# One PSUM sum for a weight gradient of two layers, more tiles turned in the forward, and turned tiles stored from SyncE, in a fused forward and backward kernel

## The chip, the cores and the metric

The kernel runs on one core of a Trainium2 chip. The metric is the device time of one execution in microseconds (us). The core has five engines that run in parallel, each with its own static stream of instructions: TensorE (PE; its weight loads are counted as PEld), VectorE (DVE), ScalarE (ACT), GpSimd (POOL) and SyncE (SP). An engine takes its instructions in order, so one that waits holds all that are behind it. A DMA is issued by an engine: SyncE and ScalarE feed a hardware queue each (q1 and q10), GpSimd the software queue q0; all use the same 16 DMA engines.

## The reference

Two kinds of layers alternate, A, B, A, B, on a sequence of S = 2048 rows and D = 448 columns; the kernel returns the output and the gradients of all inputs.

```python
kv = shift_conv(k, shift_k) * v                     # layer A, kv is the same in both A layers
y  = irfft(rfft(kv) * rfft(ssm_k)) + kv * ssm_D     # causal convolution over the sequence
A(q) = q * y
B(x) = silu(x @ w1) @ w2                            # layer B, w1 448 x 1792, w2 1792 x 448
x = A_q
x = x + A(layernorm(x));  x = x + B(layernorm(x))   # B here: "layer 1", L == 0 in the code
x = x + A(layernorm(x));  x = x + B(layernorm(x))   # B here: "layer 2", L == 1 in the code
out = x;  grads = vjp(grad_out)                     # of A_q, A_k, A_v, A_shift_k, A_ssm_k, A_ssm_D, w1, w2
```

The gradient of w2 (gw2, output 8) is silu(h)^T times the gradient that arrives at the layer, summed over layers 1 and 2; gw1 (output 7) is the gradient of h, transposed, times the normalised input, summed over both layers as well.

## The kernel before, in words

The width F = 1792 is cut into 14 blocks of 128 (`NF`), the sequence into 16 blocks of 128 (`NT`) and, in the layers, into four chunks of 512 rows.

1. `_ssm_prefix` (to about 103 us) makes the convolution by Fourier transforms written as matmuls and stores the spectra in DRAM.
2. `Main.run` does the layers. For each chunk `h` makes h in two halves of seven blocks (L556), ScalarE makes tanh and silu from it (L560, L561), and VectorE and ScalarE make the slope dT (L566 to L570; for layer 2 the complement of the tanh term is made by the activation at L566, for layer 1 by VectorE). `out` multiplies by w2 (ps_o, L588). Layer 2 goes straight on to its backward: `g_pre` turns grad_out (gb loaded by SyncE), `ga` multiplies by w2 transposed (ps_g, L618) and makes ghT on ScalarE and VectorE (L624, L625), and `gn` multiplies by w1 transposed (ps_n, L659) and makes the layernorm's backward. When all four chunks of layer 2 are through, layer 1's backward follows chunk by chunk, with dTl, nb_l and na_l loaded by SyncE (`load_l0`).
3. `_ln` makes the layernorms: VectorE takes the statistics (L257 to L262, ln_ve last), GpSimd takes rstd from it (L264), VectorE makes ln_nmr (L266) and ScalarE the normalised rows (na, nb, L271). TensorE turns them (ps_t, L503).
4. silu(h), aT in the code, and ghT are kept for the weight gradients. They lie with the width on the partitions, but are wanted there with the sequence on the partitions. There are two ways. `store_plain` (L484) stores the tile as it is, from GpSimd, and the transpose is made when it is loaded again (`dma_start_transpose` in `_load_stat`). `store_turned` (L476 to L481) turns the tile in the forward with two DMA transposes from SyncE (of four and three blocks, L480) into `turned` (two buffers), and GpSimd stores that (L481). Half 0 of layer 1 is stored plain, half 1 and both halves of layer 2 turned; of ghT layer 1 plain, layer 2 turned.
5. `_wgrad_w2_first` makes layer 1's part of gw2: per block 16 matmuls (ps_d, L795) of a loaded stat tile (dstat) and mov2, the layer's gradient. ScalarE copies the sum (dpo, L804) and GpSimd stores it in fp32 in W2P_d (L805). Ten blocks are placed at the end of `Main`, four in the next stage.
6. `_ssm_suffix` makes the convolution's backward: stage 1 of the transform (ps_s, L209, with the constants M1s, loaded at L852 by GpSimd), transposes (ps_tr, L873), the product with the spectra per part cp = 0 to 6 (`spectrum`, `kernel_part`, `inverse`; kk_c holds the loaded spectra, L229 and L230 are the inverse transform), and the gradients gK, gkv, and gk. It ends at about 731 us. `kernel_part` also loads ksf (1.8 MB, at cp 2) and mov3 (1.8 MB, at cp 4).
7. `_wgrad_rest` makes layer 2's part of gw2 (its moving operand grad_out, dmov, loaded by SyncE) and adds the part in W2P_d to it (dpart, L816; DVE, L821), and then gw1: per block 32 matmuls, a copy (dout, L826), transposes (ps_dt) and a scaled copy (do7, L831).

A tile scheduler decides the static order of every engine when the kernel is built, from priorities and a cost model. Work of `_wgrad_w2_first` and `_wgrad_rest` has a low priority and so fills TensorE's gaps in the convolution's backward; `issue_after` sets only the earliest place. A tile with a `tag` and `bufs=n` takes one of n places in turn, and so waits for the last reader of what was there before. The PSUM banks are "mm" (two of two banks), "tr" (two) and "po" (two).

## Time and profile before

| what | value |
|---|---|
| median of 8 executions | 829.93 us (828.0 to 841.82) |
| the profiled execution | 836.9 us, span 835.1 us, mean granted TensorE clock 0.97 |
| software queue q0 (GpSimd) | 92.99 MB, 34.0% of 16 engines' span |
| stores of A_d and GH_d from turned (GpSimd) | 12 and 8, of 896 KB |
| loads of dstat from A_d (SyncE) | 21, of 512 KB, median 8.2 us to landing |
| ps_d, second products (L795, with dmov) | 448 matmuls, 99.0 us, mean 356 ns |
| last ps_n matmul, VectorE's end of the layers | 547.1 us, about 563.6 us |
| convolution's backward ends, gw1 | about 731 us, 736.9 to 830 us |

The page gives the busy time of each engine, the span in 40 slices, the DMA queues, a chain of work that ended last, and groups of instructions by line. A line of the timeline reads: start, length, engine, source line, operation, result<-operands, shape, count, and in brackets the idle time before and what ended it. The waits view gives for each engine and line what it waited for: us in total, times, longest. Times come from one execution.

### The profile page before, as it was taken

How to read it: one execution, taken by the hardware profiler on the slowest of the kernel's cores; microseconds unless marked ns; L12 is line 12 of the kernel's file. 1: busy time of each engine (PE TensorE's matmuls, PEld its weight loads, DVE VectorE, ACT ScalarE, POOL GpSimd, SP SyncE). 2: the span in 40 equal slices, each digit the busy share in tenths (PEclk: the TensorE clock that was granted, in tenths of full speed). 3: DMA queues.
4: the chain of work that ended last, by engine and by line, in shares of the span. 5: the costliest groups of instructions: out<-in, count | busy, mean ns of one | idle time of the engine just before them, and what ended most of it. 6: DMA issues, size and time to landing. Idle time of an engine off the chain costs nothing.

```text
span 835.1 us, 12887 instructions
## 1 busy us (share of the span) xinstructions
PE 759.1 (91%) x4921; PEld 414.3 (50%) x4950; DVE 570.1 (68%) x1252; ACT 455.5 (55%) x577; POOL 152.6 (18%) x225
## 2 busy tenths in 40 slices
PE   6998788999997989969999999998879899989997
PEld 4966443444443444424444444454546585445553
DVE  4789677999863896986968999992465467701000
ACT  4789776787956858568855533323435563200100
POOL 1143222232111012011101001112111142311111
PEclk9999898999998999989999999999998999999999
DMA  9269898776787759958799556499888969797771
GB/s 320 110 207 274 326 231 210 231 240 202 194 159 178 176 154 201 153 176 220 221 269 272 205 171 199 118 260 302 296 260 291 348 252 193 207 273 180 188 177 42
DMA packets 168875, 181.36 MB, mean 217 GB/s; under 512 B 135456, under 2 KB 139168, under 8 KB 167662
## 3 DMA queue, kind: packets, MB, share of 16 engines
q1 hardware_dynamic: 144768, 83.54, 41.2%
q0 software_dynamic: 22304, 92.99, 34.0%
q10 hardware_dynamic: 1742, 4.02, 2.1%
q8 instruction: 38, 0.62, 0.3%
q14 instruction: 23, 0.19, 0.1%
HBM read 69.85 MB, written 70.19 MB: 168 GB/s over the span
## 4 chain that ended last, share of the span: by engine, by line
issue 26%; DVE 23%; PE 19%; ACT 13%; DMA 12%; POOL 6%; SPq 0%; POOLq 0%; ACTq 0%; DVEq 0%
PE ps_d L795 4%; DMA out_dram<-gKD 3%; DVE lb_u L642 3%; DVE X L643 3%; DMA turned<-aT 2%; DVE lb_junk L639 2%; ACT aT L561 2%; PE ps_g L618 2%; DMA KB<-Z 2%; ACT dT L560 2%; ACT dT L566 2%; POOL rstd L264 2%; DMA dstat<-A_d 2%; ACT nb L271 2%; DVE dT L570 2%
## 5 line engine op out<-in xcount | busy, mean ns | idle before, releaser
L795 PEld LDWEIGHTS <-dstat 128*128 128x128 bf16 x896 | 87.1, 98 | 88.7 <-issue 7.5
L618 PE MATMUL ps_g<-gT,w2T 128*128 128x512 bf16 x432 | 103.3, 389 | 14.1 <-ACT ghT L624 13.0
L556 PE MATMUL ps_h<-nT,w1sb 112*128 112x512 bf16 x448 | 107.0, 385 | 4.1 <-ACT aT L561 2.5
L795 PE MATMUL ps_d<-dmov,dstat 128*128 128x448 bf16 x448 | 99.0, 356 | 7.3 <-DMA dstat<-A_d 4.7
L659 PE MATMUL ps_n<-w1T,ghT 128*128 128x448 bf16 x448 | 91.3, 352 | 5.7 <-ACT lb_u L661 3.7
L588 PE MATMUL ps_o<-w2sb,aT 128*128 128x448 bf16 x448 | 93.7, 355 | 1.5 <-DVE X L589 1.0
L795 PE MATMUL ps_d<-mov,dstat 128*128 128x448 bf16 x448 | 92.6, 355 | 0.2 <-DMA dstat<-A_d 0.2
L618 PEld LDWEIGHTS <-w2T 128*128 128x128 bf16 x448 | 44.6, 100 | 69.4 <-issue 21.2
L556 PEld LDWEIGHTS <-w1sb 112*128 112x128 bf16 x448 | 44.1, 99 | 58.7 <-issue 13.9
L624 ACT CAST ghT<-ps_g 128x1024 bf16<-128x1024 f32 (+1 forms) x64 | 55.9, 904 | 30.2 <-PE ps_g L618 25.5
L560 ACT ACTIVATE dT<-ps_h 128x1024 bf16<-128x1024 f32 (+1 forms) x64 | 59.1, 923 | 22.4 <-PE ps_h L556 21.5
L659 PEld LDWEIGHTS <-ghT 128*128 128x128 bf16 x448 | 42.7, 98 | 49.3 <-issue 6.1
L826 DVE CAST dout<-ps_d 128x448 bf16<-128x448 f32 x14 | 8.7, 625 | 83.4 <-PE ps_d L795 83.4
L588 PEld LDWEIGHTS <-aT 128*128 128x128 bf16 x448 | 42.9, 98 | 43.8 <-ACT aT L561 4.2
L561 ACT ACTIVATE aT<-ps_h 128x1024 bf16<-128x1024 f32 (+1 forms) x64 | 59.3, 926 | 0.0
L831 ACT ACTIVATE do<-ps_dt 112x512 bf16<-112x512 bf16 x14 | 8.4, 597 | 90.2 <-PE ps_dt L829 90.2
L229 PE MATMUL ps_v<-Gsb,pa 128*128 128x128 bf16 x336 | 45.5, 229 | 7.9 <-DVE pa L439 4.0
L661 ACT ACTIVATE lb_u<-ps_n,rhalf 128x448 f32<-128x448 f32 x32 | 20.5, 640 | 51.9 <-DVE gYb L669 22.0
L230 PE MATMUL ps_v<-Gsb,pb 128*128 128x128 bf16 x336 | 44.3, 229 | 2.2 <-DVE pb L440 1.6
L569 DVE TENSOR_TENSOR w1p<-w1p,aT 128x1024 bf16<-128x1024 bf16 (+1 forms) x64 | 39.6, 618 | 6.9 <-ACT aT L561 6.0
L570 DVE TENSOR_TENSOR dT<-w1p,dT 128x1024 bf16<-128x1024 bf16 (+1 forms) x64 | 39.5, 617 | 3.5 <-ACT dT L566 3.3
L566 ACT ACTIVATE dT<-dT 128x1024 bf16<-128x1024 bf16 (+1 forms) x32 | 30.6, 964 | 18.1 <-DVE lb_cc L641 17.8
(193 smaller groups left out, 1324.5 us busy)
## 6 DMA issues: line engine op xcount, KB each, us to landing
A_d<-turned POOLq DMA_DIRECT2D x12, 896.0 KB, 5.4
dstat<-A_d SPq DMA_DIRECT2D x21, 512.0 KB, 8.2
DT_d<-dT POOLq DMA_DIRECT2D x8, 896.0 KB, 5.2
GH_d<-turned POOLq DMA_DIRECT2D x8, 896.0 KB, 6.6
dTl<-DT_d SPq DMA_DIRECT2D x8, 896.0 KB, 6.4
GH_d<-ghT POOLq DMA_DIRECT2D x8, 896.0 KB, 7.1
dstat<-GH_d SPq DMA_DIRECT2D x14, 512.0 KB, 3.6
spec_K<-Z POOLq DMA_DIRECT2D x7, 512.0 KB, 7.8
```

What stands on the lines that cost most here:

```text
L229: nc.tensor.matmul(pv[:, i, :], lhsT=pa[:, i * P:(i + 1) * P], rhs=k.Gsb[:, ga, :], start=True, stop=False)
L230: nc.tensor.matmul(pv[:, i, :], lhsT=pb[:, i * P:(i + 1) * P], rhs=k.Gsb[:, gb, :], start=False, stop=True)
L556: nc.tensor.matmul(ps[:, u, :], lhsT=self.w1sb[:, dc, ft * P:(ft + 1) * P], rhs=nT[:DC, dc, :], start=(dc == 0), stop=(dc == ND - 1))
L560: nc.scalar.activation(tm, ps[:, 0:n, :], ACT.Tanh, scale=-0.5)
L561: nc.scalar.activation(a, ps[:, 0:n, :], ACT.Silu)
L566: nc.scalar.activation(tm, tm, ACT.Copy, scale=-1.0, bias=1.0)
L570: nc.vector.tensor_tensor(out=tm, in0=wv, in1=tm, op=ALU.add)
L588: i = nc.tensor.matmul(po[:, :D], lhsT=aT[ft // 7][0][:, ft % 7, tl * P:(tl + 1) * P], rhs=self.w2sb[:, ft, :], start=(ft == 0), stop=(ft ...
L618: nc.tensor.matmul(ps[:, u, :], lhsT=self.w2T[:, b, ft * P:(ft + 1) * P], rhs=gT[:, b, :], start=(b == 0), stop=(b == ND - 1))
L624: nc.scalar.copy(v, ps[:, u[0]:u[0] + len(u), :])
L659: nc.tensor.matmul(pn[:, :D], lhsT=ghT[ft // 7][:, ft % 7, tl * P:(tl + 1) * P], rhs=self.w1T[:, ft, :], start=(ft == 0), stop=(ft == NF - 1))
L795: nc.tensor.matmul(ps[:, :D], lhsT=st[:, t, :], rhs=movs[gi][:, t, :], start=(gi == 0 and t == 0), stop=(gi == len(groups) - 1 and t == NT ...
```

## The change: what it does

- The first store of layer 1's silu(h) keeps only four blocks plain; the other ten of the fourteen are turned in the forward (seven before). Half 0 of layer 1 is now stored as four plain blocks and one turned piece of three.
- `store_turned` issues its store from SyncE, right behind its transposes, and no longer from GpSimd.
- gw2 of both layers is one PSUM sum. The DRAM tile W2P_d, the copies, stores, loads and the addition are gone. A class `Wgrad` loads the stats of the four plain blocks while the layers still run (`open`, called twice in layer 1's backward), makes their layer 1 part at the end of `Main` (`hold`) and keeps the four sums in the banks "tr" and "po" until `w2` goes on with layer 2's part. The other ten blocks make both parts one after the other.
- grad_out for gw2 (mov1) is loaded on ScalarE's queue into the place of w2T; M1s and the odd kk_c and gK2 go into the place of w1T.
- ksf is loaded at cp 6 instead of cp 2, into the place "WB" instead of one of its own; mov3 and dmov give way to two movn tiles, loaded by GpSimd just ahead of gw1. gk has two buffers instead of three, dout three instead of four, do7 one instead of two, dstat (dp) three instead of two.
- The fourth thing that the change is said to do, layer 2's slope complement on ScalarE, has no line in the diff: L566 stands in both kernels.

The diff, cut to its core:

```diff
-    k.A0_d = (dram.tile([NF // 2, P, S], ...), dram.tile([P, NF // 2, NT, P], ...))
+    k.A0_d = (dram.tile([4, P, S], ...), dram.tile([P, NF - 4, NT, P], ...))
-    k.W2P_d = dram.tile([F, D], FP32, name="W2P_d")
...
+            k.mov1 = k.wt.tile([P, NT, D], BF16, name="mov1", tag="w2T")
+            nc.scalar.dma_start(out=k.mov1[:], in_=_pm(k.grad_out[0]))
+            k.M1sb = k.wt.tile([P, 16, 2, P], BF16, name="M1s", tag="w1T")
+            nc.gpsimd.dma_start(out=k.M1sb[:].rearrange("p a c k -> p (a c k)"), in_=k.m1_h.ap())
             with tc.issue_after(k.d0_load.ins):
-                _wgrad_w2_first(k, m.td, range(10))
+                k.wg.hold()
...
-        nc.gpsimd.dma_start(out=dst[:, 7 * hh:7 * hh + 7, 4 * c:4 * c + 4, :], in_=an[:])
+        nc.sync.dma_start(out=dst[:, f0 + lo:f0 + hi, 4 * c:4 * c + 4, :], in_=an[:, lo:hi])
...
-            self.store_plain(k.A0_d[0], aT, c, 0)
+            self.store_plain(k.A0_d[0], aT, c, 0, 4)
+            self.store_turned(k.A0_d[1], aT, c, 4, 7, -4)
...
+            if c < 2:
+                k.wg.open(self.td)
...
+    def stat(self, pool, tag, bufs, src, ft):
+        if pool is None or self.job % (bufs + 3) < 3:
+            st = k.dp.tile([P, NT, P], BF16, name="dstat", tag="dstat", bufs=3)
+        else:
+            st = pool.tile([P, NT, P], BF16, name="dstat", tag=tag, bufs=bufs)
+        self.job += 1
+        _load_stat(k, st, src, ft)
...
+    def open(self, pool):
+        for _ in range(2):
+            self.stats.append(self.stat(pool, "S", 2, self.k.A0_d, len(self.stats)))
+    def hold(self):
+        for ft, st in enumerate(self.stats):
+            ps = self.k.psum.tile([P, 512], FP32, name="ps_d", tag=("tr", "po")[ft // 2], bufs=2)
+            self.last = _wmm(self.k, ps, st, self.k.mov2, True, False)
+            self.held.append(ps)
+    def w2(self, pool, mov):
+        for ft in range(NF):
+            if ft < 4:
+                ps = self.held[ft]
+            else:
+                ps = self.k.psum.tile([P, 512], FP32, name="ps_d", tag="tr", bufs=2)
+                _wmm(k, ps, self.stat(pool, "dstat", 3, k.A0_d, ft), k.mov2, True, False)
+            _wmm(k, ps, self.stat(pool, "dstat", 3, k.A_d1, ft), mov, False, True)
+            o = pool.tile([P, D], BF16, name="dout", tag="dout", bufs=3)
+            nc.vector.tensor_copy(o[:], ps[:, :D])
...
-                if cp == 2:
+                if cp == 6:
                     tc.keep_in_program_order(nc.gpsimd.dma_start(out=ksf[:], in_=_pm(k.KS_d[:])))
-                if cp == 4:
-                    tc.keep_in_program_order(nc.gpsimd.dma_start(out=mov3[:], in_=_pm(k.N_d[3][:])))
...
-            gk = p2.tile([P, 2, D], BF16, name="gk", tag="gk", bufs=3)
+            gk = p2.tile([P, 2, D], BF16, name="gk", tag="gk", bufs=2)
...
-        _wgrad_rest(k, dp2, after, mov3)
+        es2.close()
+        with tc.issue_after(k.wg.last):
+            k.wg.w2(dp2, k.mov1)
+        p3 = pool("sp3")
+        mov = [p3.tile([P, NT, D], BF16, name=f"movn{i}") for i in range(2)]
+        for L in (1, 0):
+            nc.gpsimd.dma_start(out=mov[L][:], in_=_pm(k.N_d[2 * L + 1][:]))
+        k.wg.w1(dp2, mov)
```

## The prediction

> **What bounds the kernel now.** I read the busy totals first, then the 40 slices, the waits, and the timeline at the few places where TensorE stands still.

> ```profile
> PE 759.1 (91%) x4921; PEld 414.3 (50%) x4950; DVE 570.1 (68%) x1252; ACT 455.5 (55%) x577; POOL 152.6 (18%) x225
> ...
> PE   6998788999997989969999999998879899989997
> ...
> PEclk9999898999998999989999999999998999999999
> ```

> TensorE is busy 759.1 of 835.1 us; no other engine passes 68%. The change issues the same matmuls (896 of ps_d in both, and as many in all), so it pays only through idle time of TensorE or through its granted clock. Three stretches matter: the layers (to 547 us, the last ps_n matmul), the backward convolution (to 731) and the closing products (to 835). Summing TensorE's gaps over short windows from 547 to 830 gives 19.96 us, the large ones below.

> ```profile
> 576.01 0.54 PE L209 MATMUL ps_s<-gYb,M1s 128*128 128x448 bf16 x2 [2.83 <-ACT A1g L111]
> 625.69 0.55 PE L795 MATMUL ps_d<-dmov,dstat 128*128 128x448 bf16 x1 [3.86 <-DMA dstat<-A_d]
> 667.15 0.29 PE L229 MATMUL ps_v<-Gsb,pa 128*128 128x128 bf16 x1 [3.74 <-DVE pa L908]
> ```

> The bracket is the idle time ahead and what ended it: an eviction, a late operand of gw2, and a vector product that itself waited for the spectrum. The rest: 3.4 us in small gaps at ps_tr (597 to 617), 1.65 at gk (723), 2.20 for dmov (745), 0.72 at the end. Each large gap is followed by a lower clock, read in 2-us windows (columns: window, length, then busy time of PE, PEld, DVE, ACT, POOL, then PEclk, DMA share, GB/s):

> ```profile
> 576.00:578.00 2.00, 1.99 (x8) 0.84 (x8) 0.52 (x1) 0.91 (x1) 0.76 (x2) 0.66 0.98 377
> 578.00:580.00 2.00, 2.00 (x7) 0.87 (x6) 0.57 (x1) 0.66 (x1) 0.00 (x0) 0.50 1.02 392
> 626.00:628.00 2.00, 1.78 (x5) 0.76 (x5) 0.00 (x0) 0.87 (x1) 0.00 (x0) 0.50 1.06 442
> 628.00:630.00 2.00, 2.00 (x9) 1.00 (x8) 0.00 (x0) 1.04 (x2) 0.00 (x0) 0.50 0.89 362
> ```

> A window of 2 us at 0.50 loses 1 us, at 0.66 0.7. So the three gaps cost about 1.7, 2.6 (to 632, the next window at 0.69) and, from 667 to 674 by the same reading (0.50, 0.50, 0.50, 0.94), 2.4 us more, 6.7 together: 19.96 + 6.7 = 26.7 us is the pool from which the tail can be paid. The DMA share is near 1 there.

> In the layers the waits show GpSimd standing behind the turned tiles (columns: us in total, times, longest):

> ```profile
> POOL A_d L481 <- DMA turned<-aT: 92.7, 10, 15.0
> POOL GH_d L481 <- DMA turned<-ghT: 59.4, 8, 10.3
> ...
> DVE ln_nmr L266 <- POOL rstd L264: 16.8, 12, 4.6
> ```

> GpSimd also computes rstd. While it waits for a transpose before storing, rstd waits behind it:

> ```profile
> 246.18 0.17 DVE L262 TENSOR_SCALAR ln_ve<-ln_mv 128x4 f32<-128x4 f32 x1
> ...
> 249.45 0.98 POOL L481 DMA_DIRECT2D A_d<-turned  x1 [6.60 <-DMA turned<-aT]
> 250.45 1.03 POOL L264 TENSOR_TENSOR rstd<-ln_ve,mhalf 128x4 f32<-128x4 f32 x1
> ...
> 252.53 0.35 PE L503 MATMUL ps_t<-ident,nb 128*112 128x128 bf16 x1 [2.22 <-ACT nb L271]
> ```

> ln_ve is ready at 246.35, rstd starts at 250.45, 4.10 us late; TensorE stands 2.22 us, then 0.30 and 1.91. The 20 us from 240 have 15.38 busy at clock 0.83.

> **Part 1: the turned store from GpSimd to SyncE.** GpSimd loses 20 waits of 152.1 us in all and 20 issues of about 0.98. At 246 all 4.10 us of lateness go, plus up to the 3.4 us of clock (20 x 0.17). Elsewhere rstd is late by 4.4 (138), 1.9 (192), 3.9 (219) and 2.6 us (322), but TensorE has work: the only gaps found are 1.51 at 155 and 0.76 at 209. High end 4.1 + 1.5 + 0.8 + 3.4 = 9.8. Low end 2, if ACT, where nb follows casts, refills the place. I take 6.

> [...] By the row the saving isn't the 0.98 us of issue but the waiting instruction ahead of rstd, and the sum is 6. [...]

> The wait doesn't vanish; it moves to SyncE. Queued there: x0c, gb, dTl, nb_l, na_l, the next transposes and gw2's loads; TensorE waits for gb (through gT), for dTl (through ghT) and for the buffers T that a transpose frees. A ghT pair was issued at 257.27 and 262.12, landed at 266.89, stored at 267.46: 10.2 us of SyncE each. A chunk of layer 2 takes about 55.5 us (ob stores at 255.40, 314.23, 369.75, 421.18), with four pairs: 40.8 us. It fits, so 0; the other end is rival 2.

> **Part 2: ten turned blocks in the forward.** Four more transposes of 12 tiles, with stores of 384 KB, in layer 1, where a chunk has one and a half pairs: 0. Removed: three of seven late transposing loads (dstat from A_d, median 7.5 us, as against 3.6 for plain). The other four move: SyncE's order puts three among the forward's last stores, where each waits for the plain store that GpSimd issues, and one later. With layer 2's pairs ahead that is covered, 0; uncovered it would cost 0 to 7.5 us once. GpSimd's plain stores shrink from 7 to 4 blocks, below nothing by under 1 us; 0.

> **Part 3: one PSUM sum for gw2.** Gone: 14 ACT copies of 0.53 us (7.4), 14 GpSimd stores (0.54 issue each) with 38.1 us of waits, 14 SyncE loads and 6.4 MB. DVE's add becomes a copy (0.62 and 0.625): even. ACT is 55% busy, so its 7.4 us are off the path: 0. What counts is the order of TensorE's work after the last ps_n. Before: 129 ps_d matmuls there, then stage 1 of the convolution. After: 16 of a held block, 4 of stage 1, 40 ps_d, then the mix. The four held blocks sit in both banks of tr and po, and po is released only when ACT has read ps_n (at 549.61 and 555.54, 0.63 each). So TensorE starts to stand at 547.1.

> *Start.* M1s lay in a place of its own (issued 540.88, landed after 7.6). It now takes w1T's, so it can't start before about 547.6 and lands near 555.2. TensorE waits for the po bank at 547.1 to about 550.2 (3.1), runs 16 matmuls of 0.2 to 550.2 + 3.1 = 553.3, then waits 1.9 for M1s. Together 5.0 of standing. Two bounds: 2, if fillers go first; 8, if M1s takes 11 us, between kk_c's median of 7.1 and its longest of 15.1.

> [...]

> *Stage 1.* Its 2.83 falls with the fillers and with A1g's evictions no longer behind the partial copies; DVE is not free before about 563.6. Left: 1.0.

> *Spectrum.* ksf (1.8 MB, issued 616.34, 17 us) leaves cp 2 for cp 6, and mov3 (642.68, 14.2 us) leaves cp 4. They shared the DMA engines with the late dstat at 625.69 and kk_c at 667.15, so these gaps (3.86, 3.74 and 5.0 of clock) go nearly whole. Left: dstat 1.5, kk_c 0.5. The bounds are 0 and the 7.6 of before. Twelve fillers inside ps_tr, none before, take 3.4 to 1.1.

> *End.* gk's buffers go from 3 to 2; a gk store takes 2.2, 4.1 and 8.0 us (least, median, most), so 1.65 becomes 3.65 (1.65 to 5.65). Both movn loads (GpSimd, 1.8 MB each) come after gk; 113 ps_d, 24 us, cover them: mov3's 14.2 for the first, 1.5 taken (0 to 4). dmov's 2.20 goes, since mov1 is loaded on ACT's queue at about 527. do7 with one buffer: 6.45 us of product per block against 0.6 of copy and a store, 0. End 0.7.

> After: 5.0 + 2.5 + 1.0 + 1.1 + 2.0 + 3.65 + 1.5 + 0.7 = 17.5. Before: 26.7. Gain 9.2.

> **Part 4: the slope complement on ScalarE.** No line of the diff carries it; the activation of layer 2 at L566 stands in both. 0, and with that a part of the title does nothing.

> **Sum.** -6 - 9.2 = -15.2. The profiled run took 836.9 us (span 835.1, 1.8 around it); it becomes 821.7. The median of eight runs is 829.93, 7.0 us (0.8%) lower. I apply the same 15.2: 814.7.

> **Rivals.**

> *1: the tail's gain comes back elsewhere.* The gap on dstat only moves: TensorE takes its operands earlier, and M1s, held back by w1T, costs the 8. Against it, ksf and mov3 did lie in both stalls. Then parts 2 and 3 give about 1.5 beside 3 of part 1: -4.5, 825.5. Chance 0.18.

> *2: SyncE stands behind its own transposes (slower).* Each store holds SyncE until its pair has landed. Four pairs per chunk of 55.5 us allow 13.9 each, other loads left aside. The slowest pair before (issued 330.05 and 334.74, landed 345.31) took 15.3, with the issue 15.8: 1.9 over. If all 16 pairs of layer 2 do so, gb, dTl and T come 30 us late: -15.2 + 30 = +15, 845. It eats the whole gain from 13.9 + 15.2/16 = 14.85 us per pair. For it: the hardware queue that SyncE feeds already takes 41.2% of all engines' time, and the longest wait on a transpose was 15.0. Against it: the usual pair takes 10.2. Chance 0.22.

> *3: nothing moves.* Part 4 does nothing already; that part 1 doesn't either would need rstd never to be waited for, which the 4.6 us above exclude.

> **How the numbers follow.** Forecast 0.60, from -8 to -22. Range: down to 803 if part 1 gives 9.8 and the tail's small terms are at their low ends (under 0.06 lie below), up to 834, into rival 2 (0.14 above). About 0.5% (4.1 us) is what a measurement of this kernel can tell from no change. Rival 1 lies half within it (0.09), rival 2 has 0.02 there and 0.20 beyond it, the forecast wholly faster: faster 0.69, same 0.11, slower 0.20.

> **What would show it.** Right: no GpSimd wait on turned; rstd directly after ln_ve; no gap at 250; stage 1 near 555 after a wait for M1s; no gap over 3 us on dstat or kk_c; no dpo or dpart. Wrong: SyncE waits on turned over 13 us with TensorE gaps on ghT or gb (rival 2); gaps of like size moved to M1s, dstat, gk or movn (rival 1).

## The result, and the profile after

The changed kernel takes 819.07 us (median of 11 runs, 814.27 to 821.64), the kernel before 830.94 us over 32 runs: ratio 0.9852 (95% interval 0.9825 to 0.9878), 11.9 us less by the medians. 814.7 was forecast, 15.2 us less. A second set of runs gave 0.9862 (0.9825 to 0.9899). The profiled execution took 820.31 us, span 818.5. The first page of the profile after answers to the three rows of before:

```profile
PE 752.0 (92%) x4921; PEld 411.4 (50%) x4950; DVE 567.8 (69%) x1252; ACT 448.3 (55%) x563; POOL 124.1 (15%) x192
...
PE   6998788999999989969999999979899997999996
...
PEclk9999899999999999989999999999999999999999
```

As many matmuls, 7.1 us less busy time and 9.5 us less idle time in the span. The mean granted clock rose from 0.97 to 0.985, and I put the shorter busy time down to it: the 16.6 us between the two spans are partly clock. The waits view shows that GpSimd no longer waits for turned at all; its other row is down from 16.8 us, and SyncE has taken the waits over (the second fence is SyncE's own waits view; columns as before):

```profile
DVE ln_nmr L271 <- POOL rstd L269: 9.4, 11, 1.2
```

```profile
SPq L487 <- DMA turned<-aT: 35.0, 15, 4.9
SPq L487 <- DMA turned<-ghT: 15.4, 7, 2.7
```

50.4 us on SyncE, at most 4.9 at a time, in place of 152.1 us on GpSimd. The timeline at the place that the prediction read (chunk 1 of layer 2) has rstd directly behind ln_ve and no gap of TensorE:

```profile
238.16 0.17 DVE L267 TENSOR_SCALAR ln_ve<-ln_mv 128x4 f32<-128x4 f32 x1
...
238.41 1.38 POOL L269 TENSOR_TENSOR rstd<-ln_ve,mhalf 128x4 f32<-128x4 f32 x1 [4.83 <-DVE ln_ve L267]
```

(The 4.83 is GpSimd's own idle time.) Rstd starts 0.08 us after ln_ve ends at 238.33. Behind the layers, the gaps of TensorE over 1 us are three, where there were seven:

```profile
541.41 4.56 PE L783 MATMUL ps_d<-mov,dstat 128*128 128x448 bf16 x16 [3.12 <-ACT lb_u L668]
```

```profile
588.47 0.23 PE L235 MATMUL ps_v<-Gsb,pb 128*128 128x128 bf16 x1 [1.98 <-DVE pb L901]
```

```profile
687.75 0.53 PE L991 MATMUL ps_gk<-gkp,ident 128*128 128x448 bf16 x1 [5.10 <-ACT gk L111]
```

These are the held block that waits for its po bank, the first part of the spectrum, and gk with its two buffers. No wait on dstat over 0.5 us is left in this execution.

### The profile page after: what moved, and what is told of

Read it like the earlier page. It is cut to its first block, busy times and chain, and to the rows that moved or that the text cites. A ratio compares the mean times of both kernels' runs of the same rounds, so it can differ in the third digit from the quotient of the medians.

```text
span 818.5 us, 12814 instructions
## 1 busy us (share of the span) xinstructions
PE 752.0 (92%) x4921; PEld 411.4 (50%) x4950; DVE 567.8 (69%) x1252; ACT 448.3 (55%) x563; POOL 124.1 (15%) x192
## 4 chain that ended last, share of the span: by engine, by line
DVE 34%; PE 25%; issue 19%; ACT 14%; DMA 5%; POOL 4%; SPq 0%; POOLq 0%; ACTq 0%; DVEq 0%
PE ps_d L783 5%; DVE lb_u L649 5%; DVE X L650 4%; DVE lb_junk L646 4%; PE ps_g L625 3%; ACT aT L567 2%; DVE lb_u L678 2%; ACT dT L572 2%; ACT dT L566 2%; PE ps_h L562 2%; DVE ghT L632 2%; DVE dT L576 2%; ACT na L276 2%; POOL rstd L269 2%; PE ps_v L235 1%
## 5 line engine op out<-in xcount | busy, mean ns | idle before, releaser
L625 PE MATMUL ps_g<-gT,w2T 128*128 128x512 bf16 x432 | 101.8, 385 | 11.6 <-ACT ghT L631 10.5
L562 PE MATMUL ps_h<-nT,w1sb 112*128 112x512 bf16 x448 | 105.0, 378 | 5.6 <-ACT aT L567 4.3
L783 PE MATMUL ps_d<-mov,dstat 128*128 128x448 bf16 x448 | 101.3, 359 | 4.4 <-ACT lb_u L668 3.7
L595 PE MATMUL ps_o<-w2sb,aT 128*128 128x448 bf16 x448 | 91.3, 352 | 0.7 <-ACT aT L567 0.3
L783 PE MATMUL ps_d<-movn,dstat 128*128 128x448 bf16 x448 | 87.0, 352 | 0.0
L625 PEld LDWEIGHTS <-w2T 128*128 128x128 bf16 x448 | 44.3, 99 | 66.0 <-issue 16.8
L566 ACT ACTIVATE dT<-ps_h 128x1024 bf16<-128x1024 f32 (+1 forms) x64 | 58.9, 921 | 16.7 <-PE ps_h L562 16.1
```

Source lines behind the costliest of these rows:

```text
L562: nc.tensor.matmul(ps[:, u, :], lhsT=self.w1sb[:, dc, ft * P:(ft + 1) * P], rhs=nT[:DC, dc, :], start=(dc == 0), stop=(dc == ND - 1))
L566: nc.scalar.activation(tm, ps[:, 0:n, :], ACT.Tanh, scale=-0.5)
L595: i = nc.tensor.matmul(po[:, :D], lhsT=aT[ft // 7][0][:, ft % 7, tl * P:(tl + 1) * P], rhs=self.w2sb[:, ft, :], start=(ft == 0), stop=(ft ...
L625: nc.tensor.matmul(ps[:, u, :], lhsT=self.w2T[:, b, ft * P:(ft + 1) * P], rhs=gT[:, b, :], start=(b == 0), stop=(b == ND - 1))
L783: i = k.nc.tensor.matmul(ps[:, :D], lhsT=st[:, t, :], rhs=mov[:, t, :], start=first and t == 0, stop=last and t == NT - 1)
```

## The experiments

For every profile I cut the span at the same two events: layers (first ps_h to the end of the last ps_n) and tail (from there to the end of the span). Within them, idle time of TensorE was summed from the timeline and clock loss from windows of 2 us, (1 - PEclk) times busy time. A profile is one execution; the ratio comes from the timed runs, each set beside runs of the kernel before on the same chip. The expectations let the tail end with TensorE's last matmul; measured so it is 4.7 to 8.6 us shorter than in the table.

| kernel | ratio to before (95%) | layers, us | tail, us |
|---|---|---|---|
| before, first profile | 1 | 436.7 | 287.8 |
| before, second profile | 1.002 (0.9991 to 1.005) | 427.4 | 286.8 |
| before, store from SyncE, first | 1.0009 (0.998 to 1.0038) | 428.8 | 293.5 |
| before, store from SyncE, second | 1.0002 (0.9979 to 1.0026) | 427.8 | 286.9 |
| before, ksf and mov3 late | 0.9977 (0.9947 to 1.0008) | 426.6 | 287.6 |
| before, no dpart | 0.9976 (0.9947 to 1.0006) | 428.8 | 287.0 |
| changed, first profile | 0.9852 (0.9825 to 0.9878) | 426.3 | 280.2 |
| changed, second profile | 0.9862 (0.9825 to 0.9899) | 426.0 | 282.8 |
| changed, store from GpSimd | 1.0055 (1.0028 to 1.0083) | 436.8 | 282.3 |
| changed, seven plain | 0.9937 (0.991 to 0.9965) | 429.2 | 283.0 |
| changed, ksf early | 0.9933 (0.9902 to 0.9964) | 426.6 | 281.9 |
| changed, two stat places | 0.9859 (0.9823 to 0.9896) | 428.0 | 276.3 |
| changed, two blocks held | 0.9993 (0.9961 to 1.0026) | 426.1 | 286.0 |
| changed, gk in four places | 0.9820 (0.9788 to 0.9852) | 426.8 | 270.9 |

**The store alone.**

```diff
-        nc.gpsimd.dma_start(out=dst[:, 7 * hh:7 * hh + 7, 4 * c:4 * c + 4, :], in_=an[:])
+        nc.sync.dma_start(out=dst[:, 7 * hh:7 * hh + 7, 4 * c:4 * c + 4, :], in_=an[:])
```

> The kernel before with one line changed: the store of the turned tiles is issued from SyncE. Theory A (GpSimd no longer stands behind transposes, so rstd is on time): the stretch from the first ps_h to the last ps_n shrinks from 436.7 us to 426 to 430, the gaps at 155 and 252 to 256 and the clock loss after them go, and the median falls by 6 to 10 us (ratio 0.988 to 0.993). Rival B (another issuer saves only its issuing time; the layers' gain came from the new order of the forward or from the extra turned blocks): no change, ratio 1.000 within 0.003. Rival C (SyncE stands behind its own transposes): slower, ratio above 1.005, with waits on gb, dTl or T.

No change, 1.0009. The waits on turned are gone and the longest of ln_nmr on rstd is 1.2 us; the layers took 428.8 us, as theory A had it, and the time did not follow. Rival B holds for the time. Its tail was long, so a second profile was taken.

> A second run of the kernel before with only the store moved to SyncE, because its first profile had the shorter layers (428.8 us) and yet a longer tail (287.5 us beside 282 to 283) with no change of order in the tail. If that tail was one execution's: layers 426 to 429, tail 282 to 284, ratio 0.990 to 0.996. If the move itself lengthens the tail: tail 286 to 288 again, ratio 0.998 to 1.004.

Again no change, 1.0002, with layers of 427.8 and a tail of 286.9 (280.8 to the last matmul, where the first profile had 287.5): the long tail was one execution's, and the short layers still bought nothing. So the layers of before cannot usually be 436.7.

**The kernel before, once more.** No edit.

> The kernel before itself, unchanged: a second profile. If the layers of 436.7 us in the first profile are what this kernel always does, they are 435 to 438 us again. If the late rstd is left to the landing times of one execution (the kernel with the late loads ran the same forward in 426.3 us), they lie between 426 and 437 us. Ratio 1.000.

427.4 us. The 436.7 of the first profile is not what this kernel always does. Its layers had 33.5 us idle and 8.7 us of clock loss; those of the second profile 30.3 and 1.9. The two other profiles with the same forward, late loads and no dpart, have 426.6 and 428.8. At the place of the first profile, ln_ve now comes while GpSimd is already storing:

```profile
239.10 0.98 POOL L481 DMA_DIRECT2D A_d<-turned  x1 [3.30 <-DMA turned<-aT]
239.12 0.17 DVE L262 TENSOR_SCALAR ln_ve<-ln_mv 128x4 f32<-128x4 f32 x1
...
240.09 1.03 POOL L264 TENSOR_TENSOR rstd<-ln_ve,mhalf 128x4 f32<-128x4 f32 x1
```

GpSimd's wait ends at 239.10, just when ln_ve is made and not 3.1 us after it, so rstd is 0.8 us late and not 4.10; TensorE has one gap of 1.83 us there (before ps_g, at 245.30) instead of 4.4. In these two executions the landing time of one transpose decides whether the wait hurts.

**The changed kernel with the store on GpSimd again.**

```diff
-        nc.sync.dma_start(out=dst[:, f0 + lo:f0 + hi, 4 * c:4 * c + 4, :], in_=an[:, lo:hi])
+        nc.gpsimd.dma_start(out=dst[:, f0 + lo:f0 + hi, 4 * c:4 * c + 4, :], in_=an[:, lo:hi])
```

> The changed kernel with the store of the turned tiles issued from GpSimd again; all else as in the change. Theory A: the waits on turned are back on GpSimd, rstd is late again, the layers take 432 to 437 us and the time rises by 6 to 10 us over the changed kernel (825 to 829, ratio to before 0.993 to 0.998). Rival B: it stays at 819 (ratio 0.985).

1.0055: about 2% over the changed kernel, more than theory A expected, with layers of 436.8. Those two ratios come from different chips. On the same chip it is 10.6 us (1.3%) slower than the changed kernel with ksf early, and its layers are 10.5 us longer than the changed kernel's (5.4 idle, 4.4 clock); so 1.3% is shown beside a profile, and the rest up to 2% is not. Both expectations took the price of the store to be the same in both kernels, and it isn't: nothing where seven blocks are turned, 1.3 to 2% where ten are. The waits and the timeline of this run, at the end of layer 1's forward:

```profile
POOL A_d L487 <- DMA turned<-aT: 96.9, 14, 13.7
```

```profile
203.75 0.16 DVE L267 TENSOR_SCALAR ln_ve<-ln_mv 128x4 f32<-128x4 f32 x1
...
206.26 0.77 POOL L487 DMA_DIRECT2D A_d<-turned  x1 [7.29 <-DMA turned<-aT]
207.05 1.03 POOL L269 TENSOR_TENSOR rstd<-ln_ve,mhalf 128x4 f32<-128x4 f32 x1
...
209.12 0.26 PE L509 MATMUL ps_t<-ident,nb 128*112 128x128 bf16 x1 [2.62 <-ACT nb L276]
```

The chain is the one that the prediction described, at another place: 14 waits instead of 10, rstd 3.1 us late, TensorE idle 2.62 us, and gaps of 1.44 and 1.54 us at two further places of layer 1 where the changed kernel has none over 0.7 (a third, 2.06 us at 130, stands in every other profile with 1.1 to 2.0). The store on SyncE is what makes the extra turning affordable.

**Seven blocks plain in the changed kernel.**

```diff
-            self.store_plain(k.A0_d[0], aT, c, 0, 4)
-            self.store_turned(k.A0_d[1], aT, c, 4, 7, -4)
+            self.store_plain(k.A0_d[0], aT, c, 0, 7)
...
-            self.store_turned(k.A0_d[1], aT, c, 0, 7, 3)
+            self.store_turned(k.A0_d[1], aT, c, 0, 7, 0)
```

> The changed kernel with seven blocks stored plain and seven turned, as before the change; four are still held. Forecast of part 2: no change (ratio 0.983 to 0.988), layers 426 us. Rival: the three late transposing loads of dstat, longer than plain ones, stall TensorE in the spectrum part by 2 to 5 us (ratio 0.989 to 0.993); or the forward without the four extra transposes is shorter by 1 to 2 us.

0.9937, so the three extra turned blocks are worth some 0.8%, about 6 us: the rival, a little under its size. On the same chip the changed kernel with two stat places, which is as fast as the changed one, is 7.3 us faster than this one. TensorE waits for the stat in stage 1, not in the spectrum:

```profile
553.86 2.09 SPq L771 DMA_TRANSPOSE dstat<-A_d  x1
...
556.13 3.32 SPq L777 DMA_DIRECT2D dstat<-A_d  x4
...
565.16 0.93 PE L782 MATMUL ps_d<-mov,dstat 128*128 128x448 bf16 x2 [6.04 <-DMA dstat<-A_d]
```

The transposing load here occupied SyncE for 2.09 us and took 6.9 to land; the four plain loads queued behind it started at 556.13 to 559.06 and landed after 9.0 to 12.2 us. The second profile of the changed kernel has a stall at the same place, 3.42 us on dstat, the first one only 0.44, so the place is marginal in both; plain loads alone took up to 12.3 us to land there. That second profile is the slowest of its six executions (819.22 us, median 813.14).

**ksf and mov3 late in the kernel before.**

```diff
-                if cp == 2:
+                if cp == 6:
                     tc.keep_in_program_order(nc.gpsimd.dma_start(out=ksf[:], in_=_pm(k.KS_d[:])))
-                if cp == 4:
+                if cp == 6:
                     tc.keep_in_program_order(nc.gpsimd.dma_start(out=mov3[:], in_=_pm(k.N_d[3][:])))
```

> The kernel before with only the loads of ksf (from cp 2) and mov3 (from cp 4) moved to cp 6. Theory A (these two loads of 1.8 MB delayed the dstat and kk_c that TensorE waited for): the gaps of 3.86 and 3.74 us fall below 1.5 each and their clock loss of about 5 us goes with them: 7 to 12 us less, ratio 0.986 to 0.992. Rival B (the gaps come from where the fillers stand in TensorE's order, or from the traffic of kk_c itself): the gaps stay, ratio 1.000 within 0.003.

0.9977, an interval that reaches 1: theory A is refuted for the stall on dstat, which stays at full size, and half refuted for kk_c (2.27 us, where other runs with before's tail have 3.12 to 5.34). What that saved came back behind it: new gaps of 1.20 us at gK and of 3.18 us at ps_sk, the latter on gks, with the two loads now issued just ahead of those of gks and kx_s.

```profile
612.99 0.56 PE L795 MATMUL ps_d<-dmov,dstat 128*128 128x448 bf16 x1 [3.85 <-DMA dstat<-A_d]
```

**ksf early in the changed kernel.**

```diff
-                if cp == 6:
+                if cp == 2:
```

> The changed kernel with the load of ksf at cp 2 again. Theory A (the load itself is what delays dstat or kk_c): a gap of 2 to 4 us with its clock loss comes back in the spectrum part, 3 to 6 us more than the changed kernel (822 to 825, ratio to before 0.989 to 0.993). Rival B (the single sum, with its other order and its own loads, is what removed the stalls): no change, 819, ratio 0.985.

0.9933, with an interval just apart from both of the changed kernel's own: near the size that theory A expected. But the changed kernel was not run on that chip, and the one profile spans 818.5 us as the changed kernel's first does. It shows no wait on dstat over 0.6 us, and of new gaps only 1.91 us on kk_c at 615.83, with about 1.5 us of clock. So the load's place may matter in the changed kernel; 3.5 us of it are seen, and the some 6 us are not shown.

**No dpart in the kernel before.** The load is left out and the addition is a copy, so layer 1's part is missing from gw2.

```diff
-        part = dp.tile([P, D], FP32, name="dpart", tag="dpart", bufs=3)
-        nc.sync.dma_start(out=part[:], in_=k.W2P_d[ft * P:(ft + 1) * P, :])
-        return part
+        return None
...
-        nc.vector.tensor_tensor(out=o[:], in0=ps[:, :D], in1=part[:], op=ALU.add)
+        nc.vector.tensor_copy(o[:], ps[:, :D])
```

> The kernel before with the 14 loads of dpart left out and the addition made a copy of the same length (layer 1's part is missing from gw2; its copies and stores stay). Theory A (the 3.2 MB of dpart beside dstat and kk_c made the stalls): the gaps of 3.3 to 3.9 and 3.7 to 5.3 us shrink by half or more, ratio 0.990 to 0.995. Rival B: the gaps stay, ratio 0.997 to 1.002.

0.9976, interval to 1.0006, and the stalls are there (3.80 on dstat, 3.12 on kk_c): rival B. This is the second kernel that shows the stall at full size with a suspect removed.

**Two stat places instead of three in the changed kernel.**

```diff
-        if pool is None or self.job % (bufs + 3) < 3:
-            st = k.dp.tile([P, NT, P], BF16, name="dstat", tag="dstat", bufs=3)
+        if pool is None or self.job % (bufs + 2) < 2:
+            st = k.dp.tile([P, NT, P], BF16, name="dstat", tag="dstat", bufs=2)
```

> The changed kernel with two places of dstat beside the three in the closing stage, as before the change, instead of three. Theory A (the third place, so an earlier load of dstat, is what took the 3.9 us stall on dstat out of the spectrum part): a stall of 2 to 4 us on dstat comes back there with its clock loss, tail 279 to 283 us instead of 274.7 to 277.3, ratio to before 0.990 to 0.995. Rival B (the order of the fillers, without the 129 ps_d ahead of stage 1, took it out): tail unchanged, ratio 0.983 to 0.988.

0.9859, as the changed kernel, with no stall on dstat: five places in turn are enough. What then is wrong with before's? Its SyncE queue at the stall shows it:

```profile
611.23 0.32 SPq L769 DMA_DIRECT2D dstat<-A_d  x1
...
616.05 0.33 SPq L769 DMA_DIRECT2D dstat<-A_d  x1
```

The second pass over gw2 uses only two places for its first four stats (`job < bridge` with bridge 4, L788), so each load waits until 16 ps_d matmuls are through: the sixteenth of the first stat ends at 611.2, of the second at 616.0, each just before the next issue. The load of 616.05 lands at 625.64, 9.6 us later, where TensorE stands until 625.69. In the changed kernel there is no second pass, and its stats go round five or six places without a break. That a bridge with more places removes the stall was not tried, so the two places are read from the trace and not shown by a run.

**Two blocks held instead of four.** The other two early stats are used when a bank of tr comes free.

```diff
-        for ft, st in enumerate(self.stats):
+        for ft, st in enumerate(self.stats[:2]):
...
-            if ft < 4:
+            if ft < 2:
                 ps = self.held[ft]
...
-                _wmm(k, ps, self.stat(pool, "dstat", 3, k.A0_d, ft), k.mov2, True, False)
+                _wmm(k, ps, self.stats[ft] if ft < 4 else self.stat(pool, "dstat", 3, k.A0_d, ft), k.mov2, True, False)
```

> The changed kernel with only two blocks held (both in tr) and the other two of the four early stats used later, in the bank that comes free. Theory A (the held blocks in po make TensorE stand after the last ps_n until ScalarE has read it): the gap of 3.12 us, the one of 0.6 to 2 us after it and the 1.0 us of clock go: 3 to 5 us less (ratio to before 0.979 to 0.982). Rival B (stage 1 then waits for M1s, which landed 5.3 us after the last ps_n, or for its own evictions): no change or up to 3 us more.

0.9993: all of the change's gain is gone. Rival B, and dearer than it thought:

```profile
540.24 1.68 PE L214 MATMUL ps_s<-gYb,M1s 128*128 128x448 bf16 x4 [5.43 <-DMA M1s<-c_m]
550.24 2.05 PE L783 MATMUL ps_d<-mov,dstat 128*128 128x448 bf16 x5 [8.32 <-DMA dstat<-A_d]
```

```profile
SPq L778 <- DVE lb_u L649: 17.9, 1, 17.9
```

The held blocks are what TensorE does while M1s is on its way, and the unused stats keep their places: in the changed kernel the last held matmul frees one at 545.98 and the next stat is loaded into it at once, while here SyncE waits 17.9 us, to 546.4, for VectorE's last work of the layers to free another. The gap of 3.12 us is the small price.

**gk in four places.** gk takes the tag of gkv, with four buffers for both and no more memory.

```diff
-            gkv = p2.tile([P, 2, D], BF16, name="gkv", tag="gkv", bufs=2)
+            gkv = p2.tile([P, 2, D], BF16, name="gkv", tag="gkv", bufs=4)
...
-            gk = p2.tile([P, 2, D], BF16, name="gk", tag="gk", bufs=2)
+            gk = p2.tile([P, 2, D], BF16, name="gk", tag="gkv", bufs=4)
```

> The changed kernel with gk in the four places that gkv leaves (one tag, bufs 4, no more memory). Theory A (gk waits for its own place, whose store is late): the gap of 5.10 us at gk and its clock loss of 1.5 us go, 4 to 6 us less than the changed kernel (ratio to before 0.978 to 0.981). Rival B (the stores before it hold the queue and the wait moves to ps_gk's bank or to the next product): less than 2 us.

810.84 us against 813.14 for the changed kernel on the same chip (0.9820 against 0.9862): 2.3 us by the medians, 3.5 by the ratios, between the two expectations. The gap at gk is gone, and no clock loss is left in the tail of the profile, which is the fastest of the six executions (807.13 us). This is the fastest kernel of the study, but its interval overlaps that of the changed one, so its lead is not settled.

**The changed kernel again.** No edit.

> The changed kernel itself, unchanged, beside the others on one chip. Both theories: ratio to before 0.982 to 0.988; the layers (first ps_h to last ps_n) 426 us as in its first profile if their length is settled by the order of the work, 430 or more if it is left to the landing times of one execution.

0.9862, layers 426.0. All nine profiles with the store on SyncE have layers of 426 to 429.2 us, of the five with it on GpSimd two have 436.7 and 436.8.

## Why the prediction was right in sign and too large in size

**Where the 11.9 us come from.** Four profiles with before's forward (before twice, late loads, no dpart) have layers of 429.9 us on average, six with the changed forward 426.6: 3.3 less. Four with before's tail (before twice, store alone twice) have 288.8, five with the changed kernel's tail or nearly so (changed twice, store on GpSimd, ksf early, two stat places) 280.7: 8.1 less. Together 11.4. The forecast had 6 and 9.2. Both averages lean on one long execution each: without before's first profile the layers differ by 1.0, without the first of the store alone the tails by 6.5. The timed runs give another path to the same end: the store alone 0, all the rest with seven plain about 5 us (0.9937), ten turned instead of seven 6 to 7 more.

**How near the sum came was partly luck.** Part 1 was put at 6 and was worth 0 in the kernel before; part 2 was put at 0 and was worth about 6. The two errors nearly cancel. By the path of the timed runs all the rest of the change, which the forecast put at 9.2, was worth about 5.

**Part 1, the step that failed.** "I take 6", read from 4.10 us of lateness at 246, and "I apply the same 15.2" to a median 7.0 us below the profiled run. The second should have warned of the first: what made that execution slower than the median lay in the layers, just where the 6 us were taken from. Its layers were 9.3 us longer than those of the second profile, 6.8 of it clock loss. The mechanism is real (it costs 1.3 to 2% where ten blocks are turned), but in the kernel before taking it out gave no time that can be measured (1.0009 and 1.0002).

**Part 2.** "That is covered, 0; uncovered it would cost 0 to 7.5 us": the cover was not there. Seven plain blocks cost some 6 us, near the upper bound. The prediction costed the late transposing loads only by their own landing, not by the plain loads that wait behind them; in the profile with seven plain the stall is 6.04 us, against 0.44 and 3.42 in the changed kernel's two. It also set 7.5 us for a transposing load against 3.6 for a plain one, but the 3.6 are the plain loads of ghT in gw1; the plain loads of silu(h), dstat from A_d, took 8.2. For the four early stats the 0 was right: no wait on them is seen.

**Part 3, term by term** (forecast, then the two profiles of the changed kernel, gap and clock together). Start with its clock: 7.5; 5.1 and 5.1. No run shows the 2.5 that the sum has for the clock after the start's two gaps: the gaps of 3.12 and 0.61 brought only 1.4 of clock. M1s was never waited for: it landed at 543.89, 5.3 us after its issue and ahead of the end of the held block. Stage 1: 1.0; 0.7 and 6.6 (3.42 on dstat and 2.9 of clock). ps_tr: 1.1; 0.3 and 0.2. Spectrum: 2.0; 4.6 and 1.7. gk: 3.65; 6.7 and 6.7, since gaps of 5.10 and 4.45 us there bring 1.6 and 2.2 of clock that I had not put. movn: 1.5; 0. End: 0.7; 0.7. Dmov's 2.20 went, but not for the reason given: the load waited for at 745 is gw1's operand (dmov from N_d, issued at 737.2), which movn replaces, and not grad_out. TensorE's idle time and clock loss in the tail together were forecast at 17.5 and are 18.0 (13.7 + 4.3) and 21.2 (14.7 + 6.5); in before 26.7 was taken, and 27.2 and 25.4 are measured. So the sum of the tail was near while its reason was wrong in one point: ksf and mov3 did not make the stall on dstat. Removing the two loads or dpart left it in place (3.85 and 3.80 us; both together were not removed), and it is gone where the single sum leaves no second pass with two places.

**Part 4** is in no line of the diff; no run tests it.

**The rivals.** Rival 2 did not come: SyncE waits for turned at most 4.9 us, and the layers are never longer. Rival 1's mechanism is seen in small: stalls move to gk (5.10 and 4.45 us) and, in one profile, to a stat in stage 1 (3.42 us).

**The clock after a gap.** The forecast put 2.5 us for two gaps, wherever they lie; in these rows the place of the gap made the difference. In all 14 profiles the granted clock is 1.00 or 0.50, and the instants at which it changed lie whole multiples of 3.41 us apart within a profile (to 2 ns). Cut into steps of that length at these instants, TensorE's rows around the same gap of 3.12 us are, in the changed kernel and in the one with gk in four places (same order up to there):

```profile
537.39:540.80 3.41, 0.91 (x5) 0.38 (x4) 3.34 (x7) 0.17 (x1) 0.55 (x1) 1.00 0.24 58
540.80:544.21 3.41, 2.80 (x8) 1.16 (x8) 3.27 (x10) 0.56 (x2) 0.00 (x0) 0.50 0.60 250
```

```profile
532.91:536.32 3.41, 1.49 (x8) 0.68 (x7) 3.31 (x8) 0.00 (x0) 0.55 (x1) 1.00 0.28 38
536.32:539.74 3.41, 2.22 (x12) 1.17 (x12) 3.31 (x10) 0.72 (x2) 0.00 (x0) 1.00 0.66 269
539.74:543.15 3.41, 1.73 (x10) 0.78 (x8) 3.32 (x8) 0.47 (x1) 0.00 (x0) 1.00 0.39 115
```

In the first, 2.51 us of the gap fall into one step, and the next step has half clock; in the second the gap straddles two steps with 1.92 and 1.20 us, and nothing is lost. The second profile of the changed kernel, on the same chip as the one in the second fence, has 2.55 us in one step and half clock again. Over all 14 profiles, a step at full clock with over 2.02 us of idle TensorE was followed by half clock in 76 of 76 cases, one with 1.46 to 2.02 in 16 of 52, one with less in none of 3048. So of the seven profiles with this gap of 3.12 us three paid nothing for it and four one step at half clock, 1.4 us in the first fence and by estimate at most 1.7 (half of 3.41). A good part of the clock loss that differs between two profiles of one kernel may be this; how much, no run tests.

## What to carry to other kernels

Before costing a stall from one profile, ask whether that execution is slower than the median, and where: a stall that hangs on the landing time of a DMA, or on a clock that dropped, may not be in the median at all (the layers of before took 436.7 us in one profile and 427.4 in the next). Price a short gap's clock as a chance, not as a sum: four of the seven profiles with the gap of 3.12 us paid for it. Price parts of a change together where one makes another affordable: a move that was worth nothing alone was worth 1.3 to 2% with ten blocks turned. When TensorE waits for a load, look first at when its place came free (here at 616.0, with the load landing 9.6 us later), and only then at what else was on the DMA engines (two loads less left 3.85 us of the stall).

## What the runs showed of the hardware that was not expected

A transposing load of a stat from A_d held SyncE for 2.09 us where it mattered and for 1.32 to 6.82 us over the 14 profiles (median 3.7, 77 loads), where a plain one of the same 512 KB held it for 0.32 in the median (511 loads). With seven blocks plain, four plain loads stood behind one, and TensorE then waited 6.04 us for a stat.
